# Fewer attention steps in the second phase, and its weight conversions queued behind activations

## Chip, cores and metric

One core of a Trainium2 chip. The metric is the device time of one execution in microseconds (us), lower is better; the kernel before has a median of 1056.67 us over three runs (1056.6 to 1059.1).

## The reference

Attention with a memory, followed by two pairs of dense layers over 2304 tokens (4 batches of 576), all in float32:

```python
scores = scale * q @ k.T ; causal mask ; a = softmax(scores) ; local = a @ v   # 4 x 8 heads, 576 x 64
q_p = elu(q) + 1 ; mem_out = (q_p @ M_prev) / (q_p @ z_prev + 1e-6)
x = g * mem_out + (1 - g) * local                # g = sigmoid(beta), one per head; x is 2304 x 512
h = x @ w1_in ;  x = softplus(h) @ w1_out        # 512 -> 2048 -> 512, "layer 0"
h = x @ w2_in ;  y = elu(h) @ w2_out             # 512 -> 2048 -> 512, "layer 1"
```

The weights arrive as 64-bit floats.

## The kernel before

The 2304 tokens are cut into five chunks of 512, 512, 448, 416 and 416 columns. For each chunk the two layers run one after the other, so that there are ten **phases** (chunk, layer): (0,0), (0,1), (1,0), (1,1), (2,0) and so on; (0,1) is the second, (1,0) the third, (1,1) the fourth phase. A phase (`ffn`, line 678) has two halves. In the first, 16 **columns** f of the hidden layer are computed: 12 matmuls (lines 690 to 692) into one PSUM tile `h`, of which there are four; then `act`, line 663; then the result is split into a rounded high part (line 695, on ScalarE, ACT) and a low part (line 696, on VectorE, DVE). In layer 1 of chunk 0 `act` is lines 670 and 671 on ACT and 672 on DVE; its tile `t` has two buffers. In the second half there are 16 **tiles** (d, u) of 12 matmuls each (lines 707 to 709), and after every fourth the result is taken out of PSUM (line 715, or line 97 in layer 1).

Each column and each tile needs a weight tile of 128 x 512, high and low part (`weights`, line 623; four buffers). The first time it is **converted** (`convert`, line 600): a raw load of 512 KB on SyncE's queue (SP, line 595) into tile `w64`; line 606 on ACT, lines 607 and 608 on DVE, the cast to the high part on ACT (line 97) and the low part on DVE (line 618). The parts are then saved to DRAM (line 583), and later chunks load them from there (line 656). So all conversions of the layer 0 weights fall into the first phase and before it, those of layer 1 (keys `1i0` to `1i15` for the columns, `1o0_0` to `1o3_3` for the tiles) into the second phase, except six that are converted once more in chunk 1. Tile `w64` shares its three buffers (pool `tri`, tag "big") with tile `qk`, which holds the queries and keys of one attention head and is loaded on GpSimd's queue (POOL, lines 190 to 194) until `prep_qk` has split it (lines 97, 238, 239).

Attention is a generator that does a small **step** at each `next`. A step issues scores (lines 343, 355, 371), their mask and exponential (332, 336), transposes on TensorE (PE, line 409) or the product with the values (456, 475). Part A covers the first 256 tokens of a batch, part B the other 320. The parts A of batches 2 and 3 take 34 steps, then come the four parts B with 30 each; step 35 begins the first of them. In part B each pair of heads takes seven steps; the two heads of the next pair are loaded in its second and third (`load_head`, line 185) and split in its sixth and seventh.

What mixes the two is the table `TUNE["order"]` (line 43): for each phase, how many steps are done per column and per tile. The loop in `tile_memory_attention_two_ffn_kernel` adds them up and calls `next(side)` whenever a whole one is due; what is left over at the end of a phase is dropped. On each engine a scheduler then orders what was written, by priorities (`tc.high_priority`) and by `tc.issue_after(ins)`, which puts a block's instructions on the engine of `ins` behind `ins` in that engine's queue. It orders issue alone: nothing waits for `ins` to finish, and other engines are not bound. Each engine works its queue off in order.

Of the kernel before, what the change touches and what calls it, by code (L numbers as in the profile page):

```python
# [10 lines left out]
ACTF = mybir.ActivationFunctionType  # L11
# [8 lines left out]
KF = DFF // 128  # L20
# [19 lines left out]
    hi='ssss ssss', lo='v', sc='vv ssv',  # L40


    order=((0, 0, 0.95, 0.95), (0, 1, 0.25, 1.0), (1, 0, 0.45, 1.6), (1, 1, 0.4, 0.9), (2, 0, 0.3, 0.8), (2, 1, 0.4, 0.7), (3, 0, 0.3, 0.8), (3, 1, 0.4, 0.7), (4, 0, 0.0, 0.0), (4, 1, 0.0, 0.0)),
)


# [12 lines left out]
def kernel(  # L59
# [15 lines left out]
    ve, se, ge, te = nc.vector, nc.scalar, nc.gpsimd, nc.tensor  # L75
# [14 lines left out]
    T = TUNE  # L90

    def f32(ap):
        return ap.bitcast(F32)

    def copy(eng, dst, src):
        if eng is se:
            se.copy(dst, src)  # L97
        else:
            eng.tensor_copy(dst, src)
# [35 lines left out]
    def x(c, k):  # L135
        return slots[SLOT[c]][k]
# [439 lines left out]
    scratch = {}  # L576
# [4 lines left out]
    def save(key, w):  # L581
        scratch[key] = dram.tile([128, 2, 4, 128], F32, name=f"s_{key}", tag=f"s_{key}")
        E[T["st"]].dma_start(scratch[key], f32(w))

    fetched, unsaved, passes = {}, [], {}
# [37 lines left out]
    def weights(src, key):  # L623
        if key in made:
            w = made.pop(key)
            unsaved.append((key, w))
        else:
            early = key.startswith("0i") and key not in scratch
            with tc.high_priority(offset=T["pri"][key in scratch]), tc.issue_after(softs[int(key[2:]) - 10]) if early else nullcontext():
                new = key not in scratch  # L630
                passes[key] = passes.get(key, 0) + 1
                w = make(src, key)
            if len(raw_loads) >= KF:
                with tc.issue_after(sync[-1]):
                    while unsaved:
                        save(*unsaved.pop(0))
            with tc.issue_after(sync[-1]):
                put()
            if new and not (key in twice and passes[key] == 1):
                unsaved.append((key, w))  # L640
        return w[:, 0], w[:, 1]
# [3 lines left out]
    def put():  # L645
        while outs:
            c, d, o = outs.pop(0)
            at = 0
            for b, c0, n in CHUNKS[c]:
                nc.sync.dma_start(out[b, d, :, c0:c0 + n], o[:, at:at + n])  # L650
                at += n

    def make(src, key, pool=None):
        w = (pool or wp).tile([128, 2, 4, 128], F32R, name="w", tag="g" if pool else "w")
        if key in scratch:
            sync.append(nc.sync.dma_start(f32(w), scratch[key]).ins)
        else:
            convert(src, key, w)
        return w

    softs = []

    def act(c, layer, f, t, h):
        if layer == 0:
            softs.append(se.activation(t, h, ACTF.Abs).ins)
            se.activation(t, t, ACTF.Exp, scale=-1.0)
            se.activation(t, t, ACTF.Ln, bias=1.0)  # L667
            ve.scalar_tensor_tensor(t, h, 0.0, t, ALU.max, ALU.add)  # L668
        elif c == 0 or c == 1 and f % 2:
            se.activation(t, h, ACTF.Relu, scale=-1.0)  # L670
            se.activation(t, t, ACTF.Exp, scale=-1.0)
            ve.scalar_tensor_tensor(t, t, -1.0, h, ALU.add, ALU.max)  # L672
        else:
            ve.tensor_scalar(t, h, 0.0, None, ALU.min)
            se.activation(t, t, ACTF.Exp)
            ve.scalar_tensor_tensor(t, t, -1.0, h, ALU.add, ALU.max)  # L676

    def ffn(c, layer):
        win, wout = ((w1i, w1o), (w2i, w2o))[layer]
        N = WIDTH[c]  # L680
        gs = []
        for f in range(KF):
            hi, lo = weights(win[f], f"{layer}i{f}")
            t = two.tile([128, 512], F32, name="t", tag="t")
            g = gp.tile([128, 2, 512], F32R, name="g", tag="g")
            h = psf.tile([128, 512], F32, name="h", tag="h")
            with tc.issue_after(marks[1, NP - 1][0]) if (c, layer) == (0, 0) and f < 4 else nullcontext():
                for k in range(KD):
                    xk = x(c, k)
                    te.matmul(h[:, :N], hi[:, k, :], xk[:, 0, :N], start=k == 0, stop=False)  # L690
                    te.matmul(h[:, :N], hi[:, k, :], xk[:, 1, :N], start=False, stop=False)  # L691
                    end = te.matmul(h[:, :N], lo[:, k, :], xk[:, 0, :N], start=False, stop=k == KD - 1)  # L692
            column[:] = [end.ins]
            act(c, layer, f, t[:, :N], h[:, :N])
            se.copy(g[:, 0, :N], t[:, :N])  # L695
            ve.tensor_sub(g[:, 1, :N], t[:, :N], f32(g)[:, 0, :N])  # L696
            gs.append(g)
            if layer and f == KF - 1:
                busy[c].add("in")
            yield  # L700
        for d in range(KD):
            h = psf.tile([128, 512], F32, name="h", tag="h")
            for u in range(4):
                hi, lo = weights(wout[d, u], f"{layer}o{d}_{u}")
                for k in range(4):
                    f = 4 * u + k
                    te.matmul(h[:, :N], hi[:, k, :], gs[f][:, 0, :N], start=f == 0, stop=False)  # L707
                    te.matmul(h[:, :N], hi[:, k, :], gs[f][:, 1, :N], start=False, stop=False)  # L708
                    end = te.matmul(h[:, :N], lo[:, k, :], gs[f][:, 0, :N], start=False, stop=f == KF - 1)  # L709
                column[:] = [end.ins]  # L710
                if u < 3:
                    yield
            if layer == 0:
                y = x(c, d)
                se.copy(y[:, 0, :N], h[:, :N])
                ve.tensor_sub(y[:, 1, :N], h[:, :N], f32(y)[:, 0, :N])
            else:
                o = two.tile([128, 512], F32, name="t", tag="t")
                copy(se, o[:, :N], h[:, :N])
                outs.append((c, d, o))  # L720
                if c == len(CHUNKS) - 1:
                    put()
            yield
# [36 lines left out]
    with tc.tile_pool(name="pre", bufs=1) as pre, tc.tile_pool(name="pre3", bufs=2) as pre3:  # L760
# [5 lines left out]
        for _ in chain(((0, "A", pre3, loads), (1, "A", pre3, None)), T["ahead"][0]):  # L766
            if k == T["pads"]:
                pads()
            if k >= begin and (k - begin) % step == 0 and len(made) < count - T["inw"]:
                key = f"0i{len(made)}"  # L770
                made[key] = make(w1i[len(made)], key, gp)
            k += 1
        with tc.issue_after(marks[1, NP - 2][1]), tc.issue_after(marks[1, NP - 2][2]):
            while len(made) < count:
                key = f"0i{len(made)}"
# [22 lines left out]
    for c, layer, *halves in T["order"]:  # L798
        while layer == 0 and not all((b, "A" if c0 < CA else "B") in ready for b, c0, _ in CHUNKS[c]):
            next(side)  # L800
        owed = 0.0
        for n, _ in enumerate(ffn(c, layer)):
            owed += halves[n // KF]
            while owed >= 1.0:
                owed -= 1.0
                with tc.high_priority(offset=400), tc.issue_after(column[0]) if c or layer else nullcontext():
                    next(side, None)
# [72 lines left out]
```

## Time and profile before

| | |
|---|---|
| median of three runs | 1056.67 us (1056.6 to 1059.1) |
| the profiled execution | 1053.93 us |
| its span | 1052.1 us |
| busy: PE, its weight loads (PEld) | 1011.3 us (96%), 897.7 us (85%) |
| busy: DVE, ACT, POOL | 672.3 us (64%), 664.5 us (63%), 104.0 us (10%) |
| chain that ended last | PE 77%, DVE 8%, DMA 6%, ACT 5%, issue 3% |
| moved by DMA | 240.27 MB, 228 GB/s on average |

The profile is that of one execution; the span is the time between its first and last instruction, and the execution's own time is 1.8 us more. The shares are averages over phases that differ: PE is full in most of them and not in all, and DVE and ACT are nearly full in some and half idle in others. So the trace is asked by stretches. The second phase lies between 178.6 us (its first matmul of a column) and 308.1 us in the span, its second half begins at 235.7 us.

### The profile page before, as it was taken

What the parts mean: (1) busy time and instruction counts of PE and PEld (TensorE: products, weight loads), DVE (VectorE), ACT (ScalarE), POOL (GpSimd) and SP (SyncE); (2) the same over time, 40 slices, a digit from 0 to 9 for tenths busy, and PEclk for the clock granted to TensorE, in tenths of its full rate; (3) what the DMA queues carried; (4) which work ended last, traced back from release to release, by engine and by line L of the source; (5) the groups of instructions that cost most, each with busy time, mean ns of one, the idle gap of its engine ahead of it and who ended that gap; (6) DMA issues with size and microseconds to landing.
All of it is one profiled execution on the core that took longest, in us unless ns stands there. A gap on an engine that the chain in (4) does not pass through costs nothing.

```text
span 1052.1 us, 15858 instructions
## 1 busy us (share of the span) xinstructions
PE 1011.3 (96%) x5249; PEld 897.7 (85%) x5249; DVE 672.3 (64%) x1701; ACT 664.5 (63%) x1518; POOL 104.0 (10%) x198
## 2 busy tenths in 40 slices
PE   6699999978989999999999999999999999999998
PEld 4477777767868888888889899999999999999998
DVE  6958887887768665798666667854665570240640
ACT  5869865877669955787679756555885440570420
POOL 7121221020111011000110011000000000000000
PEclk9899999999999999999999999999999999999999
DMA  8558888975786466566775666666755567777675
GB/s 245 166 207 311 288 293 299 336 264 197 232 288 223 160 203 203 177 221 227 259 245 184 223 221 215 191 233 213 234 189 172 175 233 243 251 235 233 235 238 171
DMA packets 71185, 240.27 MB, mean 228 GB/s; under 512 B 10288, under 2 KB 15552, under 8 KB 71104
## 3 DMA queue, kind: packets, MB, share of 16 engines
q1 hardware_dynamic: 62272, 207.65, 58.2%
q0 software_dynamic: 8832, 31.61, 9.8%
q8 instruction: 42, 0.69, 0.3%
q14 instruction: 39, 0.32, 0.1%
HBM read 200.95 MB, written 38.27 MB: 227 GB/s over the span
## 4 chain that ended last, share of the span: by engine, by line
PE 77%; DVE 8%; DMA 6%; ACT 5%; issue 3%; SPq 0%; ACTq 0%; DVEq 0%
PE h L707 12%; PE h L709 12%; PE h L708 12%; PE h L690 10%; PE h L692 10%; PE h L691 10%; DMA w<-in_w2o 3%; PE tp L409 3%; PE o L456 2%; PE s L343 2%; DMA w<-in_w2i 1%; PE s L355 1%; DVE wr L608 1%; DVE w L618 1%; DVE sph L332 1%
## 5 line engine op out<-in xcount | busy, mean ns | idle before, releaser
L690 PE MATMUL h<-x,w 128*128 128x512 f32 (+2 forms) x640 | 240.7, 378 | 8.3 <-DVE t L672 7.4
L707 PE MATMUL h<-g,w 128*128 128x512 f32 (+2 forms) x640 | 241.7, 378 | 0.3 <-ACT w L97 0.2
L709 PE MATMUL h<-g,w 128*128 128x512 f32 (+2 forms) x640 | 239.2, 374 | 0.5 <-DVE w L618 0.5
L708 PE MATMUL h<-g,w 128*128 128x512 f32 (+2 forms) x640 | 238.9, 373 | 0.0
L692 PE MATMUL h<-x,w 128*128 128x512 f32 (+2 forms) x640 | 238.3, 373 | 0.0
L691 PE MATMUL h<-x,w 128*128 128x512 f32 (+2 forms) x640 | 238.3, 373 | 0.0
L690 PEld LDWEIGHTS h<-x,w 128*128 128x128 f32 x640 | 120.9, 189 | 24.5 <-DVE t L672 9.4
L709 PEld LDWEIGHTS h<-g,w 128*128 128x128 f32 x640 | 121.2, 189 | 13.2 <-DVE w L618 1.1
L707 PEld LDWEIGHTS h<-g,w 128*128 128x128 f32 x640 | 121.2, 189 | 13.1 <-ACT w L97 0.7
L692 PEld LDWEIGHTS h<-x,w 128*128 128x128 f32 x640 | 120.7, 189 | 13.7 <-issue 0.2
L691 PEld LDWEIGHTS h<-x,w 128*128 128x128 f32 x640 | 121.0, 189 | 12.0
L708 PEld LDWEIGHTS h<-g,w 128*128 128x128 f32 x640 | 121.3, 190 | 10.9
L696 DVE TENSOR_TENSOR g<-t,g 128x512 fp32r<-128x512 f32 (+2 forms) x160 | 100.9, 634 | 32.2 <-ACT g L695 30.6
L695 ACT CAST g<-t 128x512 fp32r<-128x512 f32 (+2 forms) x160 | 91.5, 574 | 33.2 <-DVE t L676 25.8
L336 ACT ACTIVATE sph<-sph,neg 128x256 f32<-128x256 f32 (+4 forms) x144 | 83.4, 580 | 32.2 <-DVE neg L332 32.0
L668 DVE SCALAR_TENSOR_TENSOR t<-h,t 128x512 f32<-128x512 f32 (+2 forms) x80 | 50.3, 635 | 65.0 <-ACT t L667 64.6
L332 DVE CUSTOM_DVE_ANT_0 sph<-s,mask 128x256 f32<-128x256 f32 (+3 forms) x112 | 56.0, 520 | 49.4 <-PE s L343 41.9
L606 ACT ACTIVATE wr<-w 128x512 f32<-128x512 f32 x70 | 46.7, 672 | 36.9 <-DMA w<-in_w2o 16.3
L409 PE MATMUL tp<-ident,sph 128*128 128x128 f32 x400 | 61.6, 278 | 8.3 <-DVE sph L385 3.6
L409 PEld LDWEIGHTS tp<-ident,sph 128*128 128x128 f32 x400 | 48.9, 144 | 16.1 <-DVE sph L385 3.9
L420 DVE TENSOR_TENSOR ptj<-tp,ptj 128x512 fp32r<-128x512 f32 (+2 forms) x80 | 40.1, 513 | 31.8 <-ACT ptj L419 25.2
L97 ACT COPY t<-h 128x512 f32<-128x512 f32 (+2 forms) x20 | 10.8, 542 | 74.4 <-PE h L709 74.3
(134 smaller groups left out, 1498.8 us busy)
## 6 DMA issues: line engine op xcount, KB each, us to landing
w<-s_0i SPq DMA_DIRECT2D x64, 512.0 KB, 4.2
w<-s_0o SPq DMA_DIRECT2D x64, 512.0 KB, 3.3
w<-s_1i SPq DMA_DIRECT2D x62, 512.0 KB, 3.5
w<-s_1o SPq DMA_DIRECT2D x60, 512.0 KB, 4.1
w<-in_w2o SPq DMA_DIRECT2D x20, 512.0 KB, 4.6
w<-in_w2i SPq DMA_DIRECT2D x18, 512.0 KB, 5.5
w<-in_w1i SPq DMA_DIRECT2D x16, 512.0 KB, 4.9
s_0i<-w SPq DMA_DIRECT2D x16, 512.0 KB, 10.5
```

The lines of the kernel that those rows point to most:

```text
L332: ve.tensor_tensor_reduce(out=dst, in0=ps, in1=m, scale=-0.125, scalar=least, op0=ALU.add, op1=ALU.min, accum_out=acc)
L336: se.activation(Pi, Pi, ACTF.Exp, scale=-1.0, bias=d["neg", n][:, i:i + 1], accum_out=sums(n, i))
L409: te.transpose(pt, sph[n % 2][:, poff(n, i) + 128 * j:poff(n, i) + 128 * j + 128], ident)
L668: ve.scalar_tensor_tensor(t, h, 0.0, t, ALU.max, ALU.add)
L690: te.matmul(h[:, :N], hi[:, k, :], xk[:, 0, :N], start=k == 0, stop=False)
L691: te.matmul(h[:, :N], hi[:, k, :], xk[:, 1, :N], start=False, stop=False)
L692: end = te.matmul(h[:, :N], lo[:, k, :], xk[:, 0, :N], start=False, stop=k == KD - 1)
L695: se.copy(g[:, 0, :N], t[:, :N])
L696: ve.tensor_sub(g[:, 1, :N], t[:, :N], f32(g)[:, 0, :N])
L707: te.matmul(h[:, :N], hi[:, k, :], gs[f][:, 0, :N], start=f == 0, stop=False)
L708: te.matmul(h[:, :N], hi[:, k, :], gs[f][:, 1, :N], start=False, stop=False)
L709: end = te.matmul(h[:, :N], lo[:, k, :], gs[f][:, 0, :N], start=False, stop=f == KF - 1)
```

## The change

The table gives other rates to the first four phases. First-time conversions on ACT are queued behind an activation of the second phase: those for column f > 2 behind the first activation of column f - 3, those for the tiles `1o0_0` to `1o0_3` behind that of column 13, 14, 15 and 15. And the second phase's activations get a higher priority (offset 300). The rest of the kernel is as before; line numbers in the changed kernel are 7 or 8 higher from line 628 on.

```diff
-    order=((0, 0, 0.95, 0.95), (0, 1, 0.25, 1.0), (1, 0, 0.45, 1.6), (1, 1, 0.4, 0.9), (2, 0, 0.3, 0.8), ...
+    order=((0, 0, 1.0, 1.15), (0, 1, 0.1, 0.3), (1, 0, 0.45, 1.8), (1, 1, 0.45, 1.05), (2, 0, 0.3, 0.8), ...
...
-            early = key.startswith("0i") and key not in scratch
-            with tc.high_priority(offset=T["pri"][key in scratch]), tc.issue_after(softs[int(key[2:]) - 10]) if early else nullcontext():
+            at = None
+            if key not in scratch and passes.get(key, 0) == 0:
+                if key.startswith("0i"):
+                    at = softs[int(key[2:]) - 10]
+                elif key.startswith("1i") and int(key[2:]) > 2:
+                    at = softs[KF + int(key[2:]) - 3]
+                elif key.startswith("1o0"):
+                    at = softs[2 * KF - 3 + min(int(key[4:]), 2)]
+            with tc.high_priority(offset=T["pri"][key in scratch]), tc.issue_after(at) if at else nullcontext():
...
         elif c == 0 or c == 1 and f % 2:
-            se.activation(t, h, ACTF.Relu, scale=-1.0)
+            softs.append(se.activation(t, h, ACTF.Relu, scale=-1.0).ins)
...
-            act(c, layer, f, t[:, :N], h[:, :N])
+            with tc.high_priority(offset=300) if (c, layer) == (0, 1) else nullcontext():
+                act(c, layer, f, t[:, :N], h[:, :N])
```

On ACT, the beginning of the second phase before the change. L606 and the L97 casts `w<-wr` are conversions, L670 and L671 the activation of a column, L715 the last result of the first phase:

```order
L97 CAST w_2102<-wr_2103 128x512
L715 CAST x0_3_100<-h_1858 128x512
L606 ACTIVATE wr_2206<-w64_2207 128x512
L97 CAST w_2143<-wr_2144 128x512
L670 ACTIVATE t_2020<-h_2022 128x512
L97 CAST w_2174<-wr_2175 128x512
L670 ACTIVATE t_2051<-h_2053 128x512
L97 CAST w_2205<-wr_2206 128x512
L671 ACTIVATE t_2020<-t_2020 128x512
L606 ACTIVATE wr_2237<-w64_2238 128x512
L671 ACTIVATE t_2051<-t_2051 128x512
```

The same place in the changed kernel (L677 and L678 are the activation, L703 the split of its result; `w64_2141` is the raw tile of column 3):

```order
L416 COPY pt_2010<-tp_2041 128x384
L677 ACTIVATE t_2057<-h_2059 128x512
L606 ACTIVATE wr_2140<-w64_2141 128x512
L678 ACTIVATE t_2057<-t_2057 128x512
L677 ACTIVATE t_2088<-h_2090 128x512
L606 ACTIVATE wr_2171<-w64_2172 128x512
L678 ACTIVATE t_2088<-t_2088 128x512
L97 CAST w_2139<-wr_2140 128x512
L703 CAST g_2058<-t_2057 128x512
L703 CAST g_2089<-t_2088 128x512
L97 CAST w_2170<-wr_2171 128x512
L677 ACTIVATE t_2119<-h_2121 128x512
```

Before, the conversions of columns 3 to 6 lie ahead of the first column's split or between its parts; now that of column 3 begins behind the first activation, and each later one behind its own.

On ACT, the second half of the second phase before the change, up to the result of d = 1 (L97 `t<-h`); L419, L304, L305, L268, L269, L432 and L446 are attention:

```order
L606 ACTIVATE wr_2940<-w64_2941 128x512
L419 CAST ptj_2575<-tp_2764 128x2x256
L304 CAST phi_2775<-tp_2771 64x320
L305 CAST phi_2776<-tp_2771 64x320
L268 ACTIVATE e_3267<-qz_3025 128x384
L432 COPY sph1_96<-tp_2816 128x128
L419 CAST ptj_2575<-tp_2816 128x256
L97 CAST w_2879<-wr_2880 128x512
L606 ACTIVATE wr_2978<-w64_2979 128x512
L97 CAST w_2939<-wr_2940 128x512
```

In the changed kernel, behind the result of d = 1 (the L97 casts `R<-qk` split the two heads of the second pair):

```order
L97 COPY t_2804<-h_2697 128x512
L606 ACTIVATE wr_2857<-w64_2858 128x512
L97 CAST w_2856<-wr_2857 128x512
L97 CAST R_3162<-qk_2735 128x960
L97 CAST R_3232<-qk_2852 128x960
L606 ACTIVATE wr_2880<-w64_2881 128x512
L336 ACTIVATE sph0_95,sm_2638<-sph0_95,neg_2639 128x576
L97 CAST w_2879<-wr_2880 128x512
L606 ACTIVATE wr_2901<-w64_2902 128x512
L606 ACTIVATE wr_2959<-w64_2960 128x512
L97 CAST w_2900<-wr_2901 128x512
L606 ACTIVATE wr_2984<-w64_2985 128x512
```

Where attention and conversions alternated, conversions now follow one another, with the two heads' split among them.

## Rows read from the trace of the kernel before

**Rows 1.** Busy time by stretch: first phase's second half, then halves of later phases.
```profile
core 0: us, PE busy (x) PEld busy (x) DVE busy (x) ACT busy (x) POOL busy (x), PEclk, DMA share, GB/s
...
120.00:178.60 58.60, 58.60 (x301) 45.66 (x302) 49.18 (x150) 39.77 (x101) 10.39 (x19) 1.00 0.84 288
178.60:235.70 57.10, 49.68 (x216) 38.66 (x214) 47.23 (x86) 44.15 (x81) 6.48 (x12) 0.97 0.86 300
235.70:308.10 72.40, 64.81 (x316) 53.18 (x314) 57.20 (x142) 49.99 (x115) 9.15 (x18) 0.95 0.70 236
308.10:361.20 53.10, 53.10 (x257) 44.32 (x256) 34.15 (x75) 47.32 (x98) 3.42 (x6) 1.00 0.61 210
361.20:420.90 59.70, 59.70 (x312) 51.10 (x311) 38.49 (x104) 35.82 (x87) 6.62 (x12) 1.00 0.59 196
420.90:481.30 60.40, 59.52 (x298) 49.42 (x296) 52.84 (x127) 48.37 (x109) 5.33 (x10) 1.00 0.64 217
...
737.90:777.80 39.90, 39.90 (x225) 39.65 (x223) 24.98 (x53) 35.16 (x83) 0.00 (x0) 1.00 0.66 222
```

**Rows 2.** Waits, second phase's first half: engine, line, releaser; total, times, longest.
```profile
PE h L690 <- DVE t L672: 7.4, 4, 4.0
```

**Rows 3.** Instruction groups on ACT, 189.0 to 241.0: busy us, mean ns, idle before.
```profile
L671 ACT ACTIVATE t<-t 128x512 f32<-128x512 f32 x16 | 9.9, 630 | 0.1
L606 ACT ACTIVATE wr<-w 128x512 f32<-128x512 f32 x14 | 9.3, 672 | 4.6 <-DMA w<-in_w2o 2.9 <-DMA w<-in_w2i 1.4 <-DVE w L618 0.2
L695 ACT CAST g<-t 128x512 fp32r<-128x512 f32 x14 | 8.7, 622 | 0.7 <-DVE t L672 0.7
L97 ACT CAST w<-wr 128x512 fp32r<-128x512 f32 x14 | 8.5, 617 | 0.3 <-PE h L692 0.3
L670 ACT ACTIVATE t<-h 128x512 f32<-128x512 f32 x14 | 8.1, 593 | 1.3 <-DVE g L696 1.3
L97 ACT CAST R<-qk 128x960 fp32r<-128x960 f32 x2 | 2.0, 990 | 1.4 <-DMA qk<-in_qk 1.4
```

**Rows 4.** The same groups on DVE, 189.0 to 241.0.
```profile
L672 DVE SCALAR_TENSOR_TENSOR t<-t,h 128x512 f32<-128x512 f32 x16 | 10.8, 683 | 0.3 <-ACT t L671 0.2
L608 DVE SCALAR_TENSOR_TENSOR wr<-w,wr 128x512 int32<-128x512 int32 x14 | 9.6, 685 | 0.1
L618 DVE TENSOR_TENSOR w<-wr,w 128x512 fp32r<-128x512 f32 x14 | 9.6, 690 | 0.5 <-ACT w L97 0.3
L696 DVE TENSOR_TENSOR g<-t,g 128x512 fp32r<-128x512 f32 x14 | 9.4, 687 | 0.6 <-ACT g L695 0.6
L607 DVE TENSOR_SCALAR wr<-wr 128x512 int32<-128x512 int32 x14 | 5.9, 424 | 4.2 <-ACT wr L606 4.1
```

**Rows 5.** Waits in the second phase's second half.
```profile
ACT wr L606 <- DMA w<-in_w2o: 9.0, 9, 1.5
...
PE tp L409 <- DVE sph L385: 3.6, 1, 3.6
...
PE tp L409 <- DVE ptj L420: 3.3, 1, 3.3
```

**Rows 6.** Timeline of SP's queue, 239 to 256: start, length, line, transfer.
```profile
240.28 0.33 SPq L595 DMA_DIRECT2D w<-in_w2o  x1
...
247.18 0.33 SPq L595 DMA_DIRECT2D w<-in_w2o  x1
...
253.74 2.58 SPq L595 DMA_DIRECT2D w<-in_w2o  x2
```

**Rows 7.** Timeline of ACT and DVE around the first of these loads.
```profile
238.34 0.68 ACT L606 ACTIVATE wr<-w 128x512 f32<-128x512 f32 x1 [0.64 <-DMA w<-in_w2o]
239.51 0.69 DVE L608 SCALAR_TENSOR_TENSOR wr<-w,wr 128x512 int32<-128x512 int32 x1
241.59 0.69 DVE L618 TENSOR_TENSOR w<-wr,w 128x512 fp32r<-128x512 f32 x1
```

**Rows 8.** DMA issues, 178 to 310: transfer, queue, count, size, median us to landing.
```profile
w<-in_w2o SPq DMA_DIRECT2D x16, 512.0 KB, 4.6
...
qk<-in_qk POOLq DMA_DIRECT2D x5, 480.0 KB, 6.4
```

More of the change, by code (lines that the diff above doesn't have):

```diff
@@ L40 @@
     hi='ssss ssss', lo='v', sc='vv ssv',
-    order=((0, 0, 0.95, 0.95), (0, 1, 0.25, 1.0), (1, 0, 0.45, 1.6), (1, 1, 0.4, 0.9), (2, 0, 0.3, 0.8), (2, 1, 0.4, 0.7), (3, 0, 0.3, 0.8), (3, 1, 0.4, 0.7), (4, 0, 0.0, 0.0), (4, 1, 0.0, 0.0)),
+    order=((0, 0, 1.0, 1.15), (0, 1, 0.1, 0.3), (1, 0, 0.45, 1.8), (1, 1, 0.45, 1.05), (2, 0, 0.3, 0.8), (2, 1, 0.4, 0.7), (3, 0, 0.3, 0.8), (3, 1, 0.4, 0.7), (4, 0, 0.0, 0.0), (4, 1, 0.0, 0.0)),
 )
```

## The prediction

> **What bounds the kernel now.** I read the busy time by stretch first, one stretch for each half of a phase; then who waits in the second phase; then the costs of single instructions there; last the transfer queue and the DMA table. The profiled execution took 1053.93 us with a span of 1052.1; the median of the runs is 1056.67, so 2.7 us more. I work the difference out on the profiled execution and set it off against the median.
>
> In [rows 1] the reader is to see that TensorE (PE) is busy all of the time in both halves of the third phase (53.10 of 53.10 and 59.70 of 59.70 us), nearly so in the fourth phase's first half (59.52 of 60.40), and far from it in the second phase: 49.68 of 57.10 us in the first half and 64.81 of 72.40 in the second. The granted clock there is 0.97 and 0.95. It has two levels, 2.4 and 1.2 GHz, and at the lower one matmuls take twice as long, so the missing shares of the clock are work lost as well: 0.03 x 57.10 = 1.7 us and 0.05 x 72.40 = 3.6 us. The second phase thus loses 7.4 + 1.7 = 9.1 us in its first half and 7.6 + 3.6 = 11.2 in its second, **20.3 us together**. Everything else on PE is work, and work stays work wherever it is moved; so the sum is made in lost time alone.
>
> Why the first half loses: [rows 2] PE waits 7.4 us, in four pieces, for the column's last activation on VectorE (DVE), which frees the PSUM bank. By [rows 1] DVE is busy 47.23 of 57.10 us there and ScalarE (ACT) 44.15. A column costs ACT 0.67 + 0.62 for the conversion and 0.59 + 0.63 + 0.62 for the activation, 3.1 us [rows 3], and DVE 0.42 + 0.69 + 0.69 and 0.68 + 0.69, 3.2 us [rows 4]. PE needs 12 matmuls a column; the 192 of a half take 53.10 - 65 x 0.12 = 45.3 us (phase three's first half without its other 65 matmuls, at the price found below), 2.8 us a column. Without one attention step, then, both helpers are slower than PE here.
>
> Why the second half loses: PE waits in [rows 5] on attention steps, whose transposes stand in its queue in order while DVE is late (3.6 and 3.3 us); and the conversions are slow. Three buffers (the pool's tag "big") serve the raw weight tiles and the attention's heads. Where two heads sit in them, one is left for weights: the loads in [rows 6] go out at 240.28, 247.18 and 253.74, each as the L608 of the tile before ends (239.51 + 0.69 = 240.20 for the first, [rows 7]). That is **6.7 us a tile through one buffer**, where PE's half has 72.40 / 16 = 4.5 us a tile. ACT waited nine times for such a load [rows 5].
>
> **The change, part by part.** No instruction is added or removed; on ACT and DVE the same ones stand in another order, and on SP and POOL the same transfers.
>
> *Price of a moved matmul.* In the third phase PE never idles; its second half issues 312 - 257 = 55 matmuls more than its first and is 59.70 - 53.10 = 6.6 us longer [rows 1]: 0.12 us each. The Trainium skill, "Perfetto Trace Analysis", section "Identifying the Most-Contended Engine", says that matmul busy time is a bad measure of PE's headroom and that the busy share of the weight loads should be taken. By that rule these halves have room (44.32 of 53.10 and 51.10 of 59.70 us of weight loads), the matmuls moved into them are free, and the time is that of rival D, 1039.2 instead of 1050.0. The trace does not agree: the 55 matmuls took their 6.6 us with that room beside them. I charge the full price.
>
> *Fewer steps in the second phase.* The rates give 30 and 20 steps in phases one and two before, 34 and 6 after. Counted in the order, the second half of phase two goes from 121 attention matmuls to 31: 90 x 0.12 = 10.8 us of PE work leave it. They do not all go to phases three and four: the fourth's first half gets 25 more, the third none, the rest spreads over the first (8) and the fifth, sixth and eighth. Between the last activation of phase two and the first of phase three DVE has 77 instructions instead of 140 and ACT 58 instead of 99. Without losses the half needs 72.4 - 11.2 - 10.8 = 50.4 us, 3.15 a tile. What is late next is weights. Six steps reach the loads of the next two heads (steps 37 and 38), but not those of the two after. I count at most two tiles that find one buffer only, each 6.7 - 3.15 = 3.6 us late, 7.1 us, of which a lead of some 2 us built up by the tiles before is taken off: **5 us lost instead of 11.2**, length 55.4. Bounds: 0, if the lead covers it; 11.2, as now.
>
> *Conversions behind activations.* In the first half, ACT now starts with the activation of column 0, where five conversions stood around it; tile f comes behind the activation of column f - 3, and the activations have priority. The wait of 7.4 us [rows 2] should go. But the work that ran ahead is now inside the half: between the activations of columns 0 and 15 the order has 2 x L607, 1 x L608, 2 x L618 and 1 x L696 more on DVE, 0.8 + 0.7 + 1.4 + 0.7 = 3.6 us, and four copies less and one L606 more on ACT. DVE needs 47.2 + 3.6 = 50.8 us, more than PE's 57.1 - 9.1 + 0.2 (two matmuls more) = 48.2. How densely DVE can be filled is not known: 100% would give 50.8; the densest stretch in [rows 1], the fourth phase's first half, has 52.84 of 60.40, 87%, which would give 58.4. I take the middle, 92%: 55.3 us, so **7.1 lost instead of 9.1**. The middle, because the order is better but two heads (a cast of 0.99 on ACT each, [rows 3], after a transfer of 6.4, [rows 8]) now stand between the weights of columns 10 and 12 and hold two buffers there.
>
> *SP and POOL.* The raw loads (4.6 us to landing [rows 8]) are not bound, only ACT's part is. On POOL the two small mask copies now stand ahead of the first two heads; they wait for the last transposes of the first attention part, which the four earlier steps bring into phase one. I take 0 for this, at worst one transfer (6.4) shifted into the second phase, which is inside the bounds above.
>
> *Four steps more in phase one.* PE idles at no point of its second half, 58.60 of 58.60 us, and DVE has 49.18 of them [rows 1]; the 8 matmuls are moved work: 0.
>
> *The later phases.* In the fourth phase's first half the order puts 146 instead of 128 instructions on DVE; by the durations of the rows' kinds some 4 us, 52.8 + 4 = 57 us against PE's 59.5 + 25 x 0.12 = 62.5. PE lost 0.9 there at 87%; I add **1.0** (bounds 0 and 4). In the seventh phase's first half ACT has 84 instead of 75, some 6 us: 35.16 + 6 = 41 beside PE's 39.9 + 10 x 0.12 = 41.1: **0.5** (0 and 2). Other halves have 10 us or more of air on both helpers: 0.
>
> *Sum:* (7.1 - 9.1) + (5.0 - 11.2) + 1.0 + 0.5 = -6.7 us. Profiled execution 1047.2, median 1056.67 - 6.7 = **1050.0 us**. A measurement of this kernel can tell about 0.3% from no change, 3.2 us, so the limits are 1053.5 and 1059.8.
>
> **The rivals.**
>
> *A, slower: the conversions pace the second half, not the attention.* The 10.8 us of matmuls leave it, but the half does not become shorter, since its tiles come through buffers that heads hold, and the matmuls are paid later. The Trainium skill, same page, section "Optimization Strategy", advises to interleave stretches with different most-contended engines; this change takes interleaved work out of the second phase. The trace gives no support for leaving it there: DVE and ACT are nearly full where it is interleaved now [rows 1]. With a half of length L the difference is (L - 72.4) + 10.8 - 2.0 + 1.5 = L - 62.1. It is slower from L = 65.3, 4.1 us a tile; with the length unchanged 1067. For it: one buffer means 6.7. Against it: four heads' loads fell into this half, two do now.
>
> *B, no change: the loop of three columns.* From the activation of column f - 3 PE has 2 x 2.8 = 5.6 us of columns until it wants tile f. The five pieces take 0.67 + 0.42 + 0.69 + 0.62 + 0.69 = 3.1 us [rows 3, 4]; with one tile in work it took 241.59 + 0.69 - 238.34 = 3.9 [rows 7]. If queues full of other work make it C, a column takes (2.8 + 0.9 + C) / 3: at C = 8 it is 3.9, the first half 62.4, and the difference -6.7 + 62.4 - 55.3 = +0.4: 1057.1. It decides from C = 7.3 on.
>
> *C, more gained:* DVE packs fully and no tile is late: 3 us lost in the whole phase, nothing later: 1056.67 - 17.3 = 1039.4.
>
> *D, moved matmuls are free:* -6.7 - 10.8: 1039.2.
>
> **How the numbers follow.** Forecast 0.54 (its own range 1044 to 1053.5), A 0.12, B 0.20, C 0.10, D 0.04. Faster: 0.54 + 0.10 + 0.04, less 0.02 for the forecast's edge: 0.66. Within 0.3%: most of B and that edge, 0.20. Slower: A and the rest of B, 0.14. The range 1041 to 1059.5 leaves out D, most of C and most of A, about 0.2.
>
> **What would show it.** Right: in the second phase's first half no wait of a matmul for the last activation, PE idle by 4 to 7 us for weights, length 53 to 57; the second half 52 to 58 us long with no wait on transposes; no idle of over 2 us added later; attention in the fourth phase's first half costing some 3 us. Wrong: raw loads 6 to 7 us apart for more than three tiles (A), ACT's conversion pieces over 7 us apart from L606 to L618 (B), or new waits on DVE in the fourth phase.

## The result, and the profile after

The changed kernel takes 1069.22 us (median of four runs, 1068.2 to 1070.42), the kernel before 1057.39 beside it (1056.6 to 1059.1): a ratio of **1.0118** with a 95% interval from 1.0091 to 1.0146. It is slower, and the forecast of 1050.0 us and its range are missed. The profiled execution took 1068.2 us with a span of 1066.3 (before 1052.1).

The busy time by stretch of the changed kernel, one stretch for each half from the first half of the second phase to the first half of the fifth, and then that of the seventh (columns as in [rows 1]):

```profile
180.10:235.30 55.20, 50.78 (x218) 38.37 (x217) 47.53 (x87) 43.83 (x81) 5.78 (x12) 0.97 0.79 272
235.30:293.90 58.60, 52.47 (x225) 40.41 (x223) 41.09 (x86) 33.79 (x66) 5.35 (x10) 0.97 0.85 294
293.90:346.80 52.90, 52.90 (x253) 43.78 (x253) 31.93 (x68) 44.36 (x89) 4.02 (x7) 1.00 0.61 208
346.80:406.60 59.80, 59.80 (x312) 51.19 (x310) 39.95 (x108) 37.41 (x91) 7.26 (x13) 1.00 0.58 194
406.60:476.30 69.70, 64.68 (x323) 54.37 (x322) 56.56 (x138) 53.14 (x125) 5.36 (x10) 0.95 0.49 172
476.30:535.20 58.90, 58.90 (x302) 50.38 (x301) 41.93 (x113) 39.16 (x90) 7.21 (x13) 1.00 0.76 250
535.20:597.30 62.10, 54.42 (x281) 49.35 (x280) 38.13 (x97) 48.34 (x114) 3.90 (x7) 0.95 0.54 183
746.00:789.10 43.10, 41.92 (x233) 40.93 (x233) 27.63 (x66) 38.37 (x87) 2.13 (x4) 1.00 0.63 217
```

The fifth phase's first half in the kernel before, which the rows ahead of the prediction do not hold, in the same view:

```profile
540.30:588.00 47.70, 47.26 (x250) 43.22 (x249) 33.10 (x78) 41.94 (x96) 3.19 (x6) 1.00 0.67 228
```

Read against [rows 1], the second phase did what it was to do: 113.8 us instead of 129.5. The third is unchanged. Then the fourth phase's first half takes 69.7 us instead of 60.4 and the fifth's 62.1 instead of 47.7, and both have idle time on PE and a lowered clock. Where PE waited (the second phase's first half, its second, the fourth's first, the fifth's first; engine, line, releaser; total, times, longest):

```profile
PE h L699 <- DVE w L618: 2.4, 3, 1.4
PE h L697 <- ACT w L97: 2.0, 3, 0.8
...
PE h L715 <- ACT w L97: 4.7, 4, 2.5
...
PE tp L409 <- DVE ptj L420: 3.2, 1, 3.2
PE tp L409 <- ACT sph L383: 1.5, 1, 1.5
...
PE h L697 <- DMA w<-s_0i: 3.6, 1, 3.6
PE h L697 <- ACT x L150: 3.1, 1, 3.1
```

The wait of 7.4 us for the last activation [rows 2] is gone; in the same half PE now waits 4.4 us for weights. What makes the kernel slower are two new stalls, far behind the second phase.

**The fifth phase waits for its input.** L150 on ACT writes the rounded part of attention's result into a phase's input. The last such cast for chunk 2, from the timeline of the kernel before:

```profile
530.17 0.54 ACT L150 CAST x<-sph 128x128 fp32r<-128x128 f32 x2
```

In the changed kernel, the same cast with PE and SP's queue around it (first column: start):

```profile
525.54 10.18 SPq L663 DMA_DIRECT2D w<-s_0i  x4
...
552.39 0.55 ACT L150 CAST x<-sph 128x128 fp32r<-128x128 f32 x2
...
552.73 1.76 PE L697 MATMUL h<-x,w 128*128 128x448 f32 x4 [3.14 <-ACT x L150]
...
556.00 0.94 SPq L663 DMA_DIRECT2D w<-s_0i  x2
...
562.22 0.44 PE L697 MATMUL h<-x,w 128*128 128x448 f32 x1 [3.62 <-DMA w<-s_0i]
```

Before, the input is there at 530.2 and the phase begins at 540.3, ten us in hand. In the changed kernel the phase begins at 535.2 and the input comes at 552.4. Until 549.3 us PE does attention and those 36 matmuls of the first four columns that read the other three pieces of the input; then it stands for 3.1 us. A second wait hangs on the first: four buffers hold weights, so the load of the fifth column goes out only at 556.0, when the first column is done, and PE waits 3.6 us for it too.

**The fourth phase stops at column 7.** Column 7's weights are one of the six tiles that are converted again in chunk 1; their raw load needs a "big" buffer. The wait for one, in SP's queue in the fourth phase's first half, before and in the changed kernel:

```profile
SPq L595 <- DVE QL L239: 5.0, 2, 3.8
```

```profile
SPq L595 <- DVE QL L239: 16.0, 2, 12.7
```

L239 is the last reader of a head's queries and keys, so the load waits for attention: 12.7 us instead of 3.8. The timeline of the changed kernel there:

```profile
430.87 0.56 DVE L239 TENSOR_TENSOR QL<-qk,R 128x384 fp32r<-128x384 f32 x1
...
431.50 0.33 SPq L595 DMA_DIRECT2D w<-in_w2i  x1
...
431.93 1.57 SPq L663 DMA_DIRECT2D w<-s_1i  x3
...
434.63 0.66 PE L409 MATMUL tp<-ident,sph 128*128 128x128 f32 x4 [1.47 <-ACT sph L383]
...
436.11 0.66 ACT L606 ACTIVATE wr<-w 128x512 f32<-128x512 f32 x1
...
439.27 1.11 PE L409 MATMUL tp<-ident,sph 128*128 128x128 f32 x4 [3.23 <-DVE ptj L420]
...
441.23 0.69 DVE L618 TENSOR_TENSOR w<-wr,w 128x512 fp32r<-128x512 f32 x1
```

The load goes out as the split ends, is converted from 436.1 on and ready at 441.9. Three loads of other columns stood behind it in SP's queue and go out right after it. Until then PE's queue has attention only, 21 instructions ahead of column 7 in its order where there were 9 (in the trace 20 of them stand in one group, where there were 5). They follow from one another through ACT and DVE, so PE idles 1.5 and 3.2 us between them.

### The profile page after: what moved, and what is told of

It reads as the page before. It is cut to its first block, busy times and chain, and to the rows that moved or that the text cites. A ratio compares the mean times of both kernels' runs of the same rounds, so it can differ in the third digit from the quotient of the medians.

```text
span 1066.3 us, 15856 instructions
## 1 busy us (share of the span) xinstructions
PE 1018.6 (96%) x5249; PEld 901.3 (85%) x5249; DVE 673.5 (63%) x1701; ACT 666.6 (63%) x1518; POOL 103.8 (10%) x198
## 3 DMA queue, kind: packets, MB, share of 16 engines
q1 hardware_dynamic: 62272, 207.65, 56.2%
## 4 chain that ended last, share of the span: by engine, by line
PE 69%; DMA 3%; DVE 3%; ACT 2%; issue 1%; SPq 0%; DVEq 0%; ACTq 0%
PE h L715 10%; PE h L717 10%; PE h L716 10%; PE h L697 9%; PE h L698 9%; PE h L699 9%; PE tp L409 3%; PE o L456 3%; PE s L343 2%; DMA w<-in_w2o 1%; PE s L355 1%; DMA w<-s_0i 1%; PE o L458 1%; PE o L459 0%; PE o L452 0%
## 5 line engine op out<-in xcount | busy, mean ns | idle before, releaser
L715 PE MATMUL h<-g,w 128*128 128x512 f32 (+2 forms) x640 | 240.1, 375 | 4.7 <-ACT w L97 4.7
L715 PEld LDWEIGHTS h<-g,w 128*128 128x128 f32 x640 | 120.5, 188 | 18.2 <-ACT w L97 6.1
L716 PEld LDWEIGHTS h<-g,w 128*128 128x128 f32 x640 | 120.8, 189 | 11.2
L703 ACT CAST g<-t 128x512 fp32r<-128x512 f32 (+2 forms) x160 | 91.2, 574 | 30.4 <-DVE t L683 19.7
L332 DVE CUSTOM_DVE_ANT_0 sph<-s,mask 128x512 f32<-128x512 f32 (+3 forms) x112 | 55.9, 520 | 41.7 <-PE s L343 33.0
L409 PE MATMUL tp<-ident,sph 128*128 128x128 f32 x400 | 63.8, 284 | 4.7 <-DVE ptj L420 3.2
L606 ACT ACTIVATE wr<-w 128x512 f32<-128x512 f32 x70 | 46.6, 669 | 30.8 <-DMA w<-in_w2o 17.5
L97 ACT COPY t<-h 128x512 f32<-128x512 f32 (+2 forms) x20 | 10.8, 540 | 75.1 <-PE h L717 75.1
```

The source lines that it names most:

```text
L332: ve.tensor_tensor_reduce(out=dst, in0=ps, in1=m, scale=-0.125, scalar=least, op0=ALU.add, op1=ALU.min, accum_out=acc)
L409: te.transpose(pt, sph[n % 2][:, poff(n, i) + 128 * j:poff(n, i) + 128 * j + 128], ident)
```

## The experiments

Lengths in us, from the first matmul of a half to that of the next, out of one profile each; the ratio is to the kernel before in the same batch of runs.

| kernel | ratio (95%) | second phase | fourth phase | fifth, first half |
|---|---|---|---|---|
| before | 1 | 57.1 + 72.4 | 60.4 + 59.0 | 47.7 |
| changed | 1.0118 (1.0091 to 1.0146) | 55.2 + 58.6 | 69.7 + 58.9 | 62.1 |
| e1: table alone | 1.0094 (1.0064 to 1.0123) | 58.0 + 54.3 | 69.9 + 58.9 | 59.1 |
| e2: conversions alone | 1.0028 (1.001 to 1.0047) | 54.3 + 79.8 | 60.8 + 59.1 | 47.5 |
| e3: changed, no late input | 1.0028 (1.0006 to 1.005) | 57.1 + 58.4 | 70.3 + 58.9 | 51.1 |
| e4: changed, higher rates | 1.0432 (1.0407 to 1.0457) | 55.4 + 59.7 | 112.3 + 90.1 | 48.3 |
| e5: priority alone | 1.001 (0.9992 to 1.0029) | 58.6 + 71.5 | 60.0 + 59.0 | 47.6 |
| e6: table, one pair more | 1.004 (1.0023 to 1.0058) | 53.8 + 64.1 | 76.7 + 59.0 | 51.0 |
| e7: e3, fewer steps in (1,1) | 1.0026 (1.0004 to 1.0049) | 56.4 + 58.7 | 71.3 + 61.1 | 51.0 |
| e8: e3, columns 7, 15 saved | 1.0076 (1.0051 to 1.0102) | 58.1 + 62.1 | 59.0 + 73.2 | 49.5 |
| e9: even rates | 0.9953 (0.9937 to 0.9969) | 55.0 + 63.5 | 63.3 + 57.9 | 43.8 |
| e10: e9, bound | 0.999 (0.9975 to 1.0005) | 56.2 + 63.8 | 63.3 + 57.9 | 43.8 |
| e11: e10, columns 7, 15 saved | 0.9922 (0.9893 to 0.9951) | 56.6 + 62.8 | 58.8 + 58.0 | 43.8 |
| e12: e11, not bound | 0.989 (0.9869 to 0.9912) | 57.7 + 58.7 | 58.9 + 57.9 | 43.9 |

### Which half of the change, and the late input

e1 is the kernel before with the changed line of the table, e2 the kernel before with the rest of the change. e3 is the changed kernel with one line other, so that the fifth phase leaves out the fourth piece of its input:

```diff
-                    xk = x(c, k)
+                    xk = x(c, 2 if (c, layer, k) == (2, 0, 3) else k)
```

> The kernel before with the new table alone: no conversion is bound and no priority is changed. Theory 1 (the table makes the kernel slower: one pair of heads less is done before phase three, the pace of a pair does not rise afterwards, and the fifth phase waits for its input): slower than before by 8 to 16 us, 1065 to 1073; the last piece of chunk 2's input is cast behind the fifth phase's first matmul, some 10 us later or more. Theory 2 (the bound conversions are what costs): within 4 us of before, 1053 to 1061.

> The kernel before with bound conversions and the priority, with the old table. Theory 1: not slower than before, 1050 to 1058, with the gain in the second phase's first half (57.1 us before, 55.1 in the changed kernel). Theory 2: slower than before by 8 us or more, 1065 and up.

> The changed kernel, but the columns of the fifth phase read the third quarter of chunk 2's input twice and the fourth not at all (this part of the result is left out), so that they need not wait for the last pair of heads. Theory 1: the fifth phase's first half falls from 62.1 us to 51 to 54, the kernel to 1057 to 1062. Rival 3 (that half is long since ScalarE is busy 0.90 of it): it stays above 59 us, the kernel at 1066 to 1070.

The table alone loses nearly all of it (1.0094 of 1.0118), with the same long halves in the fourth and fifth phase; the wait in SP's queue is the same to the tenth (16.0, longest 12.7). The conversions alone lose a little, 0.1 to 0.5%, and in one place, the second phase's second half; with 1059.1 us they miss the 1058 of theory 1, and theory 2 by far. e3 takes away the late input alone, and the fifth phase's first half is 51.1 us with 0.2 of idle:

```profile
537.30:588.40 51.10, 50.95 (x280) 47.26 (x279) 37.02 (x95) 46.30 (x113) 3.73 (x7) 1.00 0.66 220
```

Rival 3 is out: ScalarE is busy 46.30 of 51.10 us here, more densely than in the changed kernel (48.34 of 62.10, 0.78 and not the 0.90 of the expectation), and the half is 11 us shorter. 1.0118 - 1.0028 = 0.9%, some 9.5 us: that is the late input's share, to within some 0.35%, as the two ratios have an interval each. The fourth phase's first half still takes 70.3.

### Why the input is late: a pair's own pace

e4 raises the rates of the third and fourth phases in the changed kernel; e6 has the changed table with 0.6 for 0.3 in the second phase, and no other part of the change:

```diff
-... (1, 0, 0.45, 1.8), (1, 1, 0.45, 1.05), ...
+... (1, 0, 0.9, 2.6), (1, 1, 0.9, 1.6), ...
```

> The changed kernel with the rates of the third phase raised from 0.45 and 1.8 to 0.9 and 2.6 and of the fourth from 0.45 and 1.05 to 0.9 and 1.6. Theory 1 (the pairs of part B follow one another at a pace of their own, 28 to 32 us a pair in the changed kernel whatever the rate): the last piece of chunk 2's input is cast at 545 us or later, the fifth phase's first half stays at 58 us or more (62.1 in the changed kernel), and the time is within 0.4% of the changed kernel's 1.0118 of before. Theory 2 (the rates decide when a pair is done): the last piece is cast before 530 us, the fifth phase's first half falls to 51 us or less, and the kernel gains some 10 us on the changed one, unless the extra steps make PE wait in the fourth phase's first half, where TensorE's order now has six products of attention with the values of the memory close together; then that half is longer than its 69.7 us and the gain is eaten.

> Before, with the changed table except that the second phase's tiles do 0.6 step each (0.3 in the changed table, 1.0 before), without the bound conversions. Theory 1 (the loss of the changed kernel is the late input of chunk 2, and every pair left out of the second phase delays it by a pair's time): with one pair more in the second phase than the changed table the last piece of chunk 2's input is cast before 535 us, the fifth phase's first half is 49 us or less, the second phase's second half lies between 58 and 68 us, and the time at 1.000 of before or less, some 0.9% under the run with the changed table alone (1.0094). Rival (the loss comes from the amount of attention in the third and fourth phases): the fourth phase's first half is 65 us or more and the fifth's 55 or more, and the time stays at 1.006 or more.

In e4 a part of the output is changed; which part was not traced. Its instructions are as many as the changed kernel's on each engine (5249 matmuls, 1701 on DVE, 1518 on ACT, 198 on POOL), so its time is read as that of the same work in another order; whether the change in the output comes with a wait less is not known.

In the timeline of the score matmuls (L343) the pairs begin, in the third phase and after, at 308, 339, 371, 401 and 433 us in e4, and at 316, 354, 384 and 415 in the changed kernel: 30 to 32 us apart at 0.9 and 2.6 steps, and 30 or 31 at 1.8. In the kernel before it was 360, 389, 419 with 1.6. So **between columns and tiles a pair takes some 30 us, seven to nine of them, at any of these rates**: its seven steps follow from one another through PE, ACT and DVE, and in PE's order the last products of two pairs are about eight tiles apart in these stretches. What sets the eight, the chain itself or the scheduler's placing of it, was not tested. A rate over 7/8 step a tile only writes steps down earlier than they are done; one well under it, the 0.45 a column, makes a pair longer (38 us from 316 to 354). One pair less in the second phase (pairs begin at 243, 274 and 308 before, at 241 and 316 after) thus delays all that follow.

Yet e4's last input came at 509 us, not at 545 or later as the theory of a fixed pace had it, and its fifth phase began without a wait (48.3). It was theory 2 that came, with its last clause: the price was paid in the fourth phase's first half:

```profile
415.40:527.70 112.30, 91.64 (x454) 76.37 (x453) 97.15 (x256) 89.16 (x216) 15.52 (x29) 0.89 0.47 150
```

Here 168 attention instructions stand ahead of column 7 in PE's order. With no columns between, three pairs begin 18 to 24 us apart (457, 475, 499), so the 30 us are the pace beside columns and tiles and not the chain's shortest, and PE waits between its links; a raw load stood 43.5 us in SP's queue, for a head's transfer. e6 says the same in small: its input is in time (534.3 against a phase that begins at 545.1, first half 51.0), but 45 instructions stand ahead of column 7, the raw load waits 22.1 us, and the fourth phase's first half takes 76.7:

```profile
SPq L595 <- DVE QL L239: 23.3, 2, 22.1
```

Its time misses the expected 1.000 by that half, 16.3 us longer than before; in this half the rival's sign came, 65 us or more, and in the fifth phase's (55 or more) it did not. The late input and the stop at column 7 are two losses.

### What stops the fourth phase: amount or place

e7 is e3 with 0.15 and 1.35 in the fourth phase instead of 0.45 and 1.05. e8 is e3 with the weights of columns 7 and 15 saved when they are first converted:

```diff
-    twice = {f"1o{d}_{u}" for d in range(KD) for u in (1,)} | {f"1i{f}" for f in (7, 15)}
+    twice = {f"1o{d}_{u}" for d in range(KD) for u in (1,)}
```

> The run in which chunk 2's columns read the third piece of their input twice and the late one not at all (part of the result left out, ratio 1.0028 there), and in the table the fourth phase's rates 0.15 per column and 1.35 per tile for 0.45 and 1.05: 4.8 steps go from its first half to its second. Theory 1 (the 9 us that the fourth phase's first half lost come from the number of attention steps beside the activations of that half): it falls from 70.3 to 63 us or less, the second half goes from 58.9 to 60 or 62, and the time falls to 0.995 to 0.998 of before. Rival (they come from where the scheduler puts a chain of transposes in TensorE's queue, whatever the rate): that half stays at 66 us or more and the time at 1.001 or more.

> The run in which chunk 2's columns read the third piece of their input twice and the late one not at all (part of the result left out, ratio 1.0028 there), and besides the weights of columns 7 and 15 of layer 1 are saved at their first conversion and loaded in chunk 1 like the others (two names leave the set twice), so that no raw load of theirs stands in SyncE's queue in the fourth phase. Theory 1 (the fourth phase's first half lost 9 us because the raw load of column 7 waits for a buffer held by the queries and keys of a pair, 12.7 us in the changed kernel, and all the attention that the rates had written ahead of it has to be done first): TensorE has no group of 21 attention instructions ahead of column 7, the half falls from 70.3 to 63 us or less with less than 1.5 us idle, the second half may take 2 us more (20 more attention instructions in it), and the time falls to 0.993 to 0.998 of before. Rival (VectorE and ScalarE, 0.81 and 0.76 busy there, pace that half): it stays at 67 us or more and the time at 1.001 or more.

e7 falls on the rival's side: with 4.8 steps fewer in it, the half takes 71.3, with the same 21 instructions ahead of column 7 and the same wait of 12.7. So the rate of this phase does not count. That what is left over from the third does is argued; the nearest test is e9 below against e6, with other rates in the third phase and nearly the same in the fourth: the raw load's wait falls from 22.1 to 5.3 us and the half from 76.7 to 63.3. e8 takes the load away, with it the second conversions of the two columns (4 instructions less on ACT, 6 on DVE), and the stop is gone. Its halves from the fourth phase's first to the fifth's first, and the load's wait in the second of them:

```profile
411.80:470.80 59.00, 59.00 (x298) 49.91 (x297) 47.31 (x112) 44.01 (x104) 3.21 (x6) 1.00 0.50 166
470.80:544.00 73.20, 68.05 (x337) 57.70 (x336) 50.92 (x142) 48.48 (x116) 9.85 (x18) 0.93 0.69 234
544.00:593.50 49.50, 49.50 (x271) 46.12 (x270) 34.70 (x86) 45.55 (x106) 3.30 (x6) 1.00 0.64 209
```

```profile
SPq L595 <- DVE QL L239: 19.7, 1, 19.7
```

The first half has no idle at all. But the second, where 61 at most was expected, takes 73.2, and the time is 1.0076 instead of 0.993 to 0.998: the next raw load is that of the second tile (`1o0_1`), and now it waits, 19.7 us, with 34 and 20 attention instructions ahead of the second and third tile in PE's order (7 and 4 in the changed kernel). The stop went to the next load of the pool. The rival that DVE and ACT pace the half is out: they are busy 0.80 and 0.75 of the first half, nearly as before the edit, and PE does not idle in it.

### Even rates, and which part of the conversions

If the pace is 7/8 step a tile, the third phase's columns, where 0.45 step a column is under the pace, are the place for a pair, and no rate should be far over one. e9 is the kernel before with such a table; e10 has it in the changed kernel; e11 adds the saved columns to e10, e12 to e9. e5 is the kernel before with the priority of the second phase's activations alone.

```diff
-... (0, 0, 0.95, 0.95), (0, 1, 0.25, 1.0), (1, 0, 0.45, 1.6), (1, 1, 0.4, 0.9), ...
+... (0, 0, 1.0, 1.15), (0, 1, 0.1, 0.6), (1, 0, 1.0, 1.0), (1, 1, 0.4, 0.9), ...
```

> Before, with other rates alone: 1.0 and 1.15 in the first phase, 0.1 and 0.6 in the second, 1.0 and 1.0 in the third, 0.4 and 0.9 in the fourth. Theory 1 (a pair takes the time of some 8 columns or tiles at any rate, and steps beyond that pile up and are called in at column 7 of the fourth phase): pairs start in the third phase's first half too, some 31 us apart, its length is 58 to 62 us (53.1 before), the fourth phase's first half is 63 us or less, the last piece of chunk 2's input is cast before the fifth phase begins, whose first half is 49 us or less, and the time is 0.994 to 1.000 of before. Rival (any shift of attention behind the second phase costs what it gains there): 1.002 or more.

> The changed kernel with the even rates of the run beside it (0.1 and 0.6 in the second phase, 1.0 and 1.0 in the third, 0.4 and 0.9 in the fourth): bound conversions and higher priority stay. Theory 1: as that run, and the bound conversions take 0 to 3 us from the second phase's first half or add as much to its second: 0.992 to 1.002 of before. Rival (the binding lengthens the second half wherever there is attention in it, as with the table of before, by 7 us): the second half 70 us or more and the time 1.003 or more.

> The run with the changed kernel and the even rates, and the weights of columns 7 and 15 saved at their first conversion. If with even rates the raw load of column 7 waits for no more than before (3.8 us there), this changes the fourth phase's first half by less than 1.5 us, and the time by less than 0.2%; if a wait of 5 us or more is left there, the half is 2 us or more shorter, and so is the time.

> Before, with the even rates (0.1 and 0.6 in the second phase, 1.0 and 1.0 in the third, 0.4 and 0.9 in the fourth) and the weights of columns 7 and 15 saved at their first conversion, without bound conversions and without the higher priority. If the binding costs as much as between the two runs with the even rates alone (0.9953 without, 0.999 with): 0.987 to 0.991 of before, below the 0.9922 of the run with binding. If that difference came from the conversions' waits of single runs: 0.991 to 0.994. The fourth phase's first half is 58 to 60 us in both cases.

> Before, with the higher priority of the second phase's activations alone (no conversion is bound behind one, the table is that of before). If the priority is what shortened the first half of the second phase in the run with the bound conversions (54.3 against 57.1 us): 54 to 55.5 us here too; if the binding did it: 57 or more. If the binding is what made its second half longer there (79.8 against 72.4 us): 71 to 74 us here, and a time 0 to 3 us under before (0.997 to 1.000); if the priority did that: 77 us or more and 1.002 or more.

e9 came out as the theory said, but for two lengths that lie 0.3 us outside their limits (57.7 for 58 to 62, 63.3 for 63 or less): pairs at 287, 317, 352 and 384, the last input at 531.4 ahead of a phase that begins at 537.4, 0.9953. What is left in the fourth phase is the raw load's wait, 5.3 us at the longest; e11 takes it away and the half is 4.5 us shorter. The version with the lowest ratio, **e12, takes 0.989 of before** and is faster than both kernels; its interval and that of e11, from another batch, overlap. Its halves from the second phase's first to the fifth's first:

```profile
178.90:236.60 57.70, 50.68 (x218) 38.76 (x216) 47.04 (x89) 43.25 (x81) 6.36 (x13) 0.97 0.91 316
236.60:295.30 58.70, 57.08 (x268) 47.25 (x269) 43.49 (x103) 40.80 (x88) 5.44 (x10) 0.97 0.77 266
295.30:353.00 57.70, 57.70 (x294) 48.63 (x292) 45.71 (x113) 54.13 (x123) 6.94 (x13) 1.00 0.62 211
353.00:410.70 57.70, 57.70 (x298) 49.24 (x297) 35.55 (x94) 34.81 (x80) 6.40 (x12) 1.00 0.57 200
410.70:469.60 58.90, 58.90 (x297) 49.87 (x296) 51.38 (x126) 48.70 (x111) 5.33 (x10) 1.00 0.61 206
469.60:527.50 57.90, 57.90 (x296) 49.13 (x295) 33.82 (x91) 30.86 (x79) 5.04 (x9) 1.00 0.68 226
527.50:571.40 43.90, 43.90 (x230) 40.52 (x229) 28.15 (x63) 38.88 (x84) 2.66 (x5) 1.00 0.64 224
```

In the last five of them PE does not idle, and the matmuls lie evenly, 294 to 298 in each half of the third and fourth phase.

Of the conversions, the priority alone does nothing (1.001; 58.6 and 71.5 us, with the wait for the last activation still 7.7). With it and the binding the second phase's second half is 79.8 us, so the binding, added to the priority, made that half longer where the table of before puts attention into it. With the even table the profiles do not agree: 63.8 us with it and 63.5 without (e10, e9), 62.8 and 58.7 with the columns saved (e11, e12). e10 is 0.4% slower than e9 in the same batch, but their two profiles differ by 0.4 us in span, so where it is lost was not found.

## Why the prediction was wrong

- **The price of a moved matmul, 0.12 us, held.** e12's third phase, first half, has 294 matmuls for 257 in [rows 1] and takes 57.7 us for 53.1, both without idle: 4.6 / 37 = 0.12. The rule of the Trainium skill ("Perfetto Trace Analysis", "Identifying the Most-Contended Engine") that rival D rested on, to judge TensorE's headroom by the busy share of weight loads, would have made them free, with weight loads at 44.32 of 53.10 us; the trace does not agree.
- **The second phase's first half** was forecast at 55.3 and took 55.2, the wait for the activation gone and PE idle 4.4 us. But this cannot be put down to the binding: over eight profiles with it the half is 54.3 to 58.1 us, over six without it 53.8 to 58.6. The gain of 1.9 us is less than what this half differs by from one profile to the next. What the binding does change is the wait: none of the eight waits for the last activation (they wait 3.9 to 6.6 us for weights), and all six without it do, 4.3 to 7.7 us, e5 with the priority alone among them. One wait took the other's place.
- **The second phase's second half**: 55.4 forecast, 58.6 measured. The step that was mis-sized is the 5 us lost: it was 6.1 of idle and 0.03 x 58.6 = 1.8 of clock, 7.9. The two tiles with one buffer were there (raw loads at 252.3, 259.4 and 265.5); the 2 us that a lead was to take off were not gained. Rivals A (65.3 us decides) and B (7.3 us from L606 to L618; 4.3 to 6.4 in the first half) did not come, nor did C (3 us lost in the whole phase; it was 6.1 + 7.9). The kernel is slower, but by no mechanism of a rival.
- **The fourth phase's first half**, "I add 1.0 (bounds 0 and 4)", is a second step that failed, a term too small: it lost 5.0 - 0.9 = 4.1 us more of idle. By the prediction's way of counting, 0.05 x 69.7 = 3.5 of clock come on top; but a lowered clock costs only while PE works, and of the 6.80 us at 0.50 PE was busy in 4.33 (last section), so it is 2.2, and **6.3 us** together. That is also what 69.7 - 60.4 leaves beside 25 matmuls at 0.12. I took DVE's fill for the only risk. DVE was busy 56.6 us as forecast (57), and that was not what bound: a raw load waited for a buffer. Of the signs of being wrong, new waits on DVE in the fourth phase came (3.2 us), as a link of that chain. I had used the shared buffers for the second phase and not asked where else a raw tile is allocated.
- **"Other halves have 10 us or more of air on both helpers: 0"** is the step that failed. The fifth phase's first half lost 7.7 - 0.5 = 7.2 of idle and 0.05 x 62.1 = 3.1 of clock, **10.3 us**. The premise did not hold by the rows either: ACT had 5.8 us of air in the third phase's first half (47.32 of 53.10 [rows 1]) and in the fifth's (41.94 of 47.70). But that was not what bound: in e3 ACT is fuller and the half loses 0.2. Air on the helpers does not say when a chain ends. Of the 32 columns and tiles of the fourth phase, the last step of chunk 2's input was written at the 23rd before and at the 28th now, and one pair takes 30 us against ten in hand. The place where it is written does not decide alone: in e9 it is the 28th too, and the input comes 7 us behind that tile's end and in time, where it is 24 us before the change and 33 in the changed kernel, which fits steps that had been written faster than they were done. I had counted which matmuls go where, not when the last of them is due.
- **The seventh phase's first half**: 0.5 forecast (0 to 2), 1.2 of idle measured.

The sum in lost time: 6.1 - 9.1 and 7.9 - 11.2 give -6.3 (forecast -8.2); 6.3 + 10.3 + 1.2 give +17.8 (forecast +1.5). The second phase begins 1.5 us later, of which 1.0 is the work of 8 moved matmuls and 0.5 loss. That is +12.0; the spans differ by 14.2. The other 2.2 us were not located: "work stays work wherever it is moved" holds here to about that much.

## What to carry to other kernels

Moving steps of a serial chain into later stretches with room costs no waiting only up to the pace that the chain has there (here 7 steps in about eight tiles): ask of every step that is moved when the last of its chain is due, and how much is in hand there. Where one pool serves two streams, each allocation is a point up to which the other stream has to be done; find all of them in the order, for steps that were written ahead are called in at the next one. Rates that are even and close to that pace (1.0 for 7/8) were worth 0.5%. Taking away such an allocation was worth another 0.6 to 0.7%, with the second conversions that go with it; in e8, where the attention stopped the next load instead, it gained nothing (1.0076 against 1.0028 for e3).

## What the hardware showed beside this

PE's granted clock fell to 0.50 (1.2 of 2.4 GHz) with each of the new stalls, for 6.8 us around the waits at 433 to 439 us and twice for 3.4 us in the fifth phase, right behind its two waits. Half of PE's busy time in these stretches is lost: 2.2 us on top of 4.1 of idle in the one half, 3.2 on top of 7.2 in the other. The stretches of the changed kernel:

```profile
436.80:443.60 6.80, 4.33 (x15) 3.88 (x16) 6.64 (x17) 4.85 (x14) 0.54 (x1) 0.50 0.70 269
552.90:556.30 3.40, 3.03 (x8) 2.21 (x9) 2.92 (x8) 3.33 (x8) 2.28 (x4) 0.50 0.64 212
563.10:566.50 3.40, 3.40 (x12) 2.94 (x11) 0.60 (x2) 0.23 (x1) 0.00 (x0) 0.50 0.35 141
```

At one order of instructions a half differs between executions where PE is not full: the second phase's first half took 55.2, 57.1 and 56.4 us in the changed kernel, e3 and e7, which do not differ up to there, while halves in which PE never idles agree within 0.2 us (52.9, 53.1 and 53.1 in the third phase's first half, 59.8 in its second each time).
